# A fused attention and softmax-gated layer on one core: float16 parts in the first product, a three-part sum handed to VectorE, and a new instruction order

## The chip, the core and the metric

The kernel runs on one core of a Trainium2 chip. The core has five engines that run side by side, each with its own in-order queue: TensorE (PE in the profile, its weight loads PEld), VectorE (DVE), ScalarE (ACT), GpSimd (POOL) and SyncE (SP), which here only issues DMAs. Engines wait for one another through semaphores. PSUM holds the results of TensorE, SBUF everything else. The metric is the device time of one execution in microseconds; lower is better. Times given are medians of several runs.

## The reference

Two layers follow each other. The first mixes seven neighbouring rows of x with softmaxed weights, one weight per head (8 heads of 24 columns) and tap; the second is a gated layer with a layer norm inside.

```python
# x: (8, 4160, 192), weight_gen: (8, 4160, 8, 7)
w = exp(weight_gen - max); w = w / (sum(w) + 1e-9)
out[b, s, h, :] = sum over k of w[b, s, h, k] * x_pad[b, s + k, h, :]
# then, on 33280 rows of 192 columns:
h = x @ w_in                                  # 192 -> 1024
e = exp(h - max(h)); sm = e / (sum(e) + 1e-9)
solu = h * sm
ln = (solu - mean) / sqrt(var + 1e-6) * g_ln
return ln @ w_out                             # 1024 -> 192
```

The weights of the second layer arrive as 64-bit floats and are turned into 32-bit ones on the chip at the start.

## The kernel before, in words

Each of 128 partitions holds a run of 260 consecutive rows, so one "tile" t is one row of each partition, 128 rows in all, and the kernel works on 260 tiles. x and the tap weights are loaded in chunks: one of 4 tiles, two of 8, then fifteen of 16 (`starts`). Four tiles make a group.

For a chunk: `load_w`, `load_x` (four DMAs, SP queue), `softmax_taps` (steps t0 to t6, line 102: max on DVE, subtraction on POOL, exponential on ACT, sum on DVE, + 1e-9 on ACT, reciprocal on DVE, product on POOL), and `norm_x` (steps v00 to v5, line 136: squares of x on ACT with their sum, then a few one-column operations that end in an upper limit for the chunk's h, used as a scale).

For a group: `attention` (line 171) runs wholly on POOL. It multiplies the seven shifted windows of x with the taps (line 174), adds parts 3, 4, 5 to 0, 1, 2 (line 180), which leaves four, and adds these pairwise into the two parts of the tile `half` (line 182; `half` has two buffers). `last_sum` (line 428) adds the two parts on DVE with a reduction (line 433) into `a`; ACT copies a piece of it (line 439).

For two tiles: TensorE transposes `a` (line 450), ACT rounds it to fp32r as `x_hi` (line 458), DVE subtracts to get the remainder `x_lo` (line 479).

For a tile: the first product (line 483) makes h, 128 x 1024, in one of three PSUM tiles named h, from high and low parts of x and w_in: x_hi·w_hi + x_hi·w_lo + x_lo·w_hi, once for the last 64 rows of w_in (line 491, `wb`, both halves of h side by side in the array) and once for the first 128 (line 494, `wa`). Then come the negated row maximum on DVE (line 505), the exponential on ACT with its sum (line 509), h·e·scale on DVE with its sum, written over h (line 515), squares on ACT (line 521), a float16 high half on ACT (line 528) and a low half on DVE (line 532), a DMA transpose (line 540), the second product in float16, 24 matmuls of 192 columns (line 580), and the scaled output on ACT (line 591). Six small steps per group (`scales`, lines 544 to 571, f0 to f5) make the output scale. The scale of h, the squares, the high half and the low half all read the same PSUM tile; it is free for the next product when squares and low half are done.

At the start three pieces of w_in and four of w_out are converted (`float_of_double`, line 232, steps a, b and c; scratch in the same three PSUM tiles h), rounded into `wa_hi`, `wa_lo`, `wb_hi`, `wb_lo` (`first_rows`, `last_rows`), and a norm of w_in is taken (`norm_of_first`, lines 282 to 299, result `column`).

The order of everything behind the first few loads comes from a planner, `issue_order` (line 660). It holds a list of steps, each with an engine, a cost in ns and the steps that it waits for, plays them through, and at each moment gives a free engine the ready step with the lowest key, the tile number plus an offset from the table `URGENCY` (line 645). The list of steps that it returns is the order in which the kernel issues its instructions; each engine then runs its own in that order.

Of the kernel before, what the change touches and what calls it, by code (L numbers as in the profile page):

```python
# [26 lines left out]
def tile_kernel(ctx: ExitStack, tc: tile.TileContext, x, weight_gen, w_in, w_out, g_ln, out):  # L27
    nc = tc.nc
# [73 lines left out]
    def softmax_taps(c, step):  # L102
# [8 lines left out]
        if step == 0:  # L111
            nc.vector.tensor_reduce(m, w3, axis=AX.X, op=ALU.max)
        elif step == 1:
            nc.gpsimd.tensor_tensor(
                out=w3, in0=w3, in1=m.unsqueeze(2).broadcast_to(wide), op=ALU.subtract
            )
        elif step == 2:
            nc.scalar.activation(w3, w3, AF.Exp)
        elif step == 3:
            nc.vector.tensor_reduce(m, w3, axis=AX.X, op=ALU.add)  # L120
        elif step == 4:
            nc.scalar.activation(y, m, AF.Copy, bias=1e-9)
        elif step == 5:
            nc.vector.reciprocal(y, y)
        elif step == 6:
            nc.gpsimd.tensor_tensor(
                out=w3, in0=w3, in1=y.unsqueeze(2).broadcast_to(wide), op=ALU.mult
            )
# [5 lines left out]
    SUM, LN, NORM, LIMIT, SCALE, EPS, EPS_Z = (slice(n, n + 1) for n in range(7))  # L134

    def norm_x(c, step, part=0):
# [12 lines left out]
        elif step == 1:  # L149
            row_of[c] = small.tile([P, 7], F32, name="row", bufs=5)  # L150
# [3 lines left out]
        elif step == 2:  # L154
            row = row_of[c]
            nc.scalar.activation(row[:, LN], row[:, SUM], AF.Ln, bias=floor)
            nc.scalar.activation(row[:, NORM], row[:, LN], AF.Exp, scale=0.5)
        elif step == 3:
            row = row_of[c]
            nc.scalar.activation(row[:, LIMIT], row[:, NORM], AF.Copy, bias=0.5, scale=column)  # L160
        elif step == 4:
            nc.vector.reciprocal(row_of[c][:, SCALE], row_of[c][:, LIMIT])
        elif step == 5:
            row = row_of[c]
            nc.scalar.activation(row[:, EPS], row[:, SCALE], AF.Copy, scale=1e-3 * FF**1.5)
            nc.scalar.activation(row[:, EPS_Z], row[:, SCALE], AF.Copy, scale=1e-12 * FF**1.5)
# [4 lines left out]
    def attention(xt, wt, t, n, half):  # L171
# [7 lines left out]
        )  # L179
        nc.gpsimd.tensor_tensor(out=pr[:, :3], in0=pr[:, :3], in1=pr[:, 3:6], op=ALU.add)  # L180
# [43 lines left out]
    minus = const.tile([P, P], F32R, name="minus")  # L224
    nc.vector.tensor_scalar_mul(minus, ident, -1.0)

    for step in range(TAP_STEPS):
        softmax_taps(0, step)
# [37 lines left out]
    wa_hi = const.tile([P, FF], F32R, name="wa_hi")  # L266
    wa_lo = const.tile([P, FF], F32R, name="wa_lo")
    wb_hi = const.tile([P, FH], F32R, name="wb_hi")
    wb_lo = const.tile([P, FH], F32R, name="wb_lo")

    def last_rows(step):
        if step < 3:
            first["b"] = float_of_double("b", raw_b, FH, step)
        elif step == 3:
            nc.scalar.copy(wb_hi, first["b"])
        elif step == 4:
            nc.vector.tensor_tensor(
                out=wb_lo, in0=first["b"], in1=wb_hi.bitcast(F32), op=ALU.subtract
            )


    def norm_of_first(step):
# [14 lines left out]
        elif step == 6:  # L297
            nc.scalar.activation(column, first["total"][:, 8:9], AF.Ln, scale=1.05 * FF)
            nc.scalar.activation(column, column, AF.Exp, scale=0.5)

    def first_rows(f, step):
# [3 lines left out]
        elif step == 3:  # L305
            nc.scalar.copy(wa_hi[:, fs], first[f])
        elif step == 4:
            nc.vector.tensor_tensor(
                out=wa_lo[:, fs], in0=first[f], in1=wa_hi.bitcast(F32)[:, fs], op=ALU.subtract
# [107 lines left out]

    def attend(t):
        n = group(t)
        c = max(n for n in range(NCHUNK) if starts[n] <= t)  # L420
        half = att.tile([P, 2, TG, D], F32, name="half", bufs=2)[:, :, :n]
        half_of[t] = half
        attention(xs[c], ws[c], t - starts[c], n, half)
# [32 lines left out]
    def high_x(t):  # L456
        hi = small.tile([P, 2, 2, P], F32R, name="x_hi", bufs=2)
# [3 lines left out]
    def subtract_high(t):  # L461

        pa, hi = x_parts[t]
        for n in range(2):
            nc.tensor.matmul(
                pa[:, n], minus, hi[:, n], start=False, stop=n == 1, skip_group_check=True
            )

    def low_x(t):
        pa, hi = x_parts.pop(t)  # L470
        lo = small.tile([P, 2, 2, P], F32R, name="x_lo", bufs=2)
        nc.scalar.copy(lo, pa)
        for i in range(2):
            xt_of[t + i] = hi[:, :, i, :], lo[:, :, i, :]

    def low_x_on_vector(t):
        pa, hi = x_parts.pop(t)
        lo = small.tile([P, 2, 2, P], F32R, name="x_lo", bufs=2)
        nc.vector.tensor_tensor(out=lo, in0=pa, in1=hi.bitcast(F32), op=ALU.subtract)  # L479
# [24 lines left out]
    def maximum(t):  # L504
        nc.vector.tensor_reduce(stat(t, NMAX), h_of[t], axis=AX.X, op=ALU.max, negate=True)  # L505

    def exponentials(t):
        e = big.tile([P, FF], F32, name="e")
        nc.scalar.activation(e, h_of[t], AF.Exp, bias=stat(t, NMAX), accum_out=stat(t, Z))  # L509
# [92 lines left out]
    def at_chunk(op, *args):  # L602
# [4 lines left out]
        xhi=high_x, xn=subtract_high, xlo=low_x, xld=low_x_on_vector, mm1=first_product,  # L607
# [21 lines left out]
    for n in range(7):  # L629
# [10 lines left out]
    for op, t in issue_order(RUN, starts, group, stat_group, LOADS):  # L640
# [19 lines left out]
def issue_order(run, starts, group, stat_group, loads):  # L660

    PE, DVE, ACT, SP, POOL = range(5)
    SAME, CROSS = (25, 127, 143, 0, 102), 130
    free = [3000, 5900, 5000, 12000, 9050]
    steps, number = [], {}  # L670

    def add(name, t, engine, cost, *after, ready=0):
        number[name, t] = len(steps)
# [4 lines left out]


    parts = ["a0", "b", "a1", *(f"c{f}" for f in range(4))]  # L680
    for n, part in enumerate(parts):
        w_in, size = n < 3, 512 if n < 3 else 384
        at = (9000, 10500, 12000)[n] if w_in else 15000
        before = () if w_in else (f"{parts[n - 3]}4", "n" + {"a0": "0", "a1": "1", "b": "2"}[parts[n - 3]]) if n < 6 else ("q00",)
        if n:
            before += (parts[n - 1] + "0",)
# [3 lines left out]
        if w_in:  # L690
            once(part + "3", ACT, 190 + 0.75 * size, part + "2")
            once(part + "4", DVE, 60 + 1.04 * size, part + "3")
            once("n" + {"a0": "0", "a1": "1", "b": "2"}[part], DVE, 60 + 1.04 * size, part + "2")
        else:
            f = n - 3
            once(f"q{f}0", ACT, 700, part + "2")
            once(f"q{f}1", PE, 660, f"q{f}0", *([f"q{f - 1}1"] if f else ["n6"]))
# [6 lines left out]
    once("n3", ACT, 100, "n0", "n1", "n2")  # L704
    once("n4", PE, 220, "n3")
    once("n5", DVE, 70, "n4")
    once("n6", ACT, 400, "n5")
# [19 lines left out]
    def add_norms(c, t):  # L727
        add("v1", t, DVE, 70, *parts_of(c), *parts_of(c - 1), ("f5", starts[c - 4] - 1 if c > 4 else -1))
        add("v2", t, ACT, 420, ("v1", t))
        add("v3", t, ACT, 190, ("v2", t), ("n6", 0))  # L730
        add("v4", t, DVE, 80, ("v3", t))
        add("v5", t, ACT, 240, ("v4", t))

    add("v00", 0, ACT, 1800, ready=9000)
    add_norms(0, 0)
    for c in range(1, len(starts) - 1):
        t, before = starts[c], starts[c - 1] if c > 1 else -1
        short = starts[c + 1] - t < 16
# [5 lines left out]
        whole = starts[c + 1] - t == 16  # L744
        for part in range(4 if whole else 1):
            size = 830 if whole else 1800
            if c > 1:

                load = min(part + 1, loads - 1) if whole else loads - 1
                add(f"v0{part}", t, ACT, size, (f"lx{load}", t))  # L750
            else:
                add(f"v0{part}", t, ACT, size, ready=15000)
        add_norms(c, t)
        n = (starts[c + 1] - t) * 8
        on = (DVE, POOL, ACT, DVE, ACT, DVE, POOL)
        wide = 60 + 7.3 * n
        costs = (wide, 13.5 * n, 100 + 6 * n, wide, 100 + n, 60 + 6.3 * n, 13.5 * n)
        for k in range(7):
            if k:
                add(f"t{k}", t, on[k], costs[k], (f"t{k - 1}", t))  # L760
            elif c > 1:
                add("t0", t, on[k], costs[k], ("lw", t), ("t6", before))
            else:
                add("t0", t, on[k], costs[k], ready=12000)

# [159 lines left out]
```

## Time and profile before

| what | value |
|---|---|
| median of 3 runs | 1348.01 us (1347.25 to 1348.76) |
| profiled execution, span from first to last instruction | 1345.8 us |
| instructions | 25810 |
| mean granted TensorE clock | 0.994 |
| 66 products of line 174 on POOL | 631.6 us |
| 66 additions of line 180 on POOL | 333.0 us |
| 66 additions of line 182 on POOL | 225.8 us |
| moved by DMA | 210.31 MB, mean 156 GB/s |

No own time is listed for the profiled execution; its span is 2.2 us below the median of the runs. In a row of the profile that groups instructions, `x64` is the count, the two numbers behind the bar are the busy time in us and the mean of one in ns, and what follows the second bar is the idle time of the engine just before them with the engine that ended it. In a row of the waits the three numbers are the total in us, how often, and the longest. In a row of the timeline the first two are start and duration in us. A row of windows gives for each engine busy us and a count, then the clock, the share of the DMA engines and GB/s.

### The profile page before, as it was taken

What the parts mean: (1) busy time and instruction counts of PE and PEld (TensorE: products, weight loads), DVE (VectorE), ACT (ScalarE), POOL (GpSimd) and SP (SyncE); (2) the same over time, 40 slices, a digit from 0 to 9 for tenths busy, and PEclk for the clock granted to TensorE, in tenths of its full rate; (3) what the DMA queues carried; (4) which work ended last, traced back from release to release, by engine and by line L of the source; (5) the groups of instructions that cost most, each with busy time, mean ns of one, the idle gap of its engine ahead of it and who ended that gap; (6) DMA issues with size and microseconds to landing.
All of it is one profiled execution on the core that took longest, in us unless ns stands there. A gap on an engine that the chain in (4) does not pass through costs nothing.

```text
span 1345.8 us, 25810 instructions
## 1 busy us (share of the span) xinstructions
PE 1246.8 (93%) x9900; PEld 970.8 (72%) x9900; DVE 1210.2 (90%) x1588; ACT 1162.8 (86%) x2318; POOL 1247.7 (93%) x241
## 2 busy tenths in 40 slices
PE   0588899999999999999999999999999999999997
PEld 0365677777777777777777777777777777777776
DVE  5988899999999999999999999999999999889994
ACT  3778889889898988989898998989898898988886
POOL 5989899999999999999999999999999999999930
PEclk9899999999999999999999999999999999999999
DMA  5277668797886889688797968878787877976776
GB/s 180 74 159 169 139 134 201 123 207 137 155 179 134 196 137 208 125 179 163 129 202 140 191 140 180 162 128 203 140 193 137 183 150 138 183 134 123 133 134 130
DMA packets 565307, 210.31 MB, mean 156 GB/s; under 512 B 544456, under 2 KB 545864, under 8 KB 565184
## 3 DMA queue, kind: packets, MB, share of 16 engines
q1 hardware_dynamic: 563208, 206.55, 75.7%
q10 hardware_dynamic: 1976, 2.12, 0.6%
q8 instruction: 78, 1.28, 0.4%
q14 instruction: 45, 0.37, 0.1%
HBM read 46.15 MB, written 25.56 MB: 53 GB/s over the span
## 4 chain that ended last, share of the span: by engine, by line
ACT 43%; DVE 35%; issue 11%; PE 7%; DMA 2%; POOL 1%; SPq 0%; ACTq 0%; POOLq 0%
ACT hl L528 12%; ACT e L521 12%; DVE h L515 11%; DVE hl L532 11%; ACT e L509 9%; DVE stats L505 5%; DVE a L433 4%; ACT junk L145 3%; PE po L580 3%; PE h L494 2%; ACT x_hi L458 2%; ACT ot L591 2%; DMA hlT<-hl 2%; PE h L491 1%; DVE x_lo L479 1%
## 5 line engine op out<-in xcount | busy, mean ns | idle before, releaser
L174 POOL TENSOR_TENSOR pr<-xt,wt 128x5376 f32<-128x5376 f32 (+1 forms) x66 | 631.6, 9569 | 2.7
L580 PE MATMUL po<-w_hl,hlT 128*128 128x192 f16 x6192 | 555.1, 246 | 17.3 <-ACT ot L591 12.6
L580 PEld LDWEIGHTS <-hlT 128*128 128x128 f16 x6240 | 505.9, 98 | 83.2 <-issue 75.5
L515 DVE SCALAR_TENSOR_TENSOR h<-h,row,e 128x1024 f32<-128x1024 f32 x260 | 333.8, 1285 | 19.1 <-ACT e L509 16.9
L528 ACT ACTIVATE hl<-h 128x1024 f16<-128x1024 f32 x260 | 266.0, 1029 | 98.4 <-DVE h L515 55.4
L532 DVE SCALAR_TENSOR_TENSOR hl<-h,hl 128x1024 f16<-128x1024 f32 x260 | 316.5, 1218 | 36.8 <-ACT e L521 34.4
L180 POOL TENSOR_TENSOR pr<-pr 128x2304 f32<-128x2304 f32 (+1 forms) x66 | 333.0, 5045 | 5.2
L505 DVE TENSOR_REDUCE stats<-h 128x1 f32<-128x1024 f32 x260 | 316.3, 1217 | 3.9 <-PE h L494 3.3
L509 ACT ACTIVATE e<-h,stats 128x1024 f32<-128x1024 f32 x260 | 293.3, 1128 | 16.1 <-DVE stats L505 15.5
L521 ACT ACTIVATE e<-h,stats 128x1024 f32<-128x1024 f32 x260 | 293.0, 1127 | 1.1 <-DVE hl L532 1.0
L494 PE MATMUL h<-wa_hi,x_hi 128*128 128x512 f32 x520 | 234.0, 450 | 0.0
L182 POOL TENSOR_TENSOR half<-pr 128x1536 f32<-128x1536 f32 (+1 forms) x66 | 225.8, 3421 | 5.2
L494 PE MATMUL h<-wa_lo,x_hi 128*128 128x512 f32 x520 | 206.4, 397 | 0.0
L494 PE MATMUL h<-wa_hi,x_lo 128*128 128x512 f32 x520 | 205.9, 396 | 0.0
L494 PEld LDWEIGHTS h<-wa_hi,x_hi 128*128 128x128 f32 x520 | 98.1, 189 | 107.1 <-issue 95.5
L491 PE MATMUL h<-wb_hi,x_hi 64*128 64x512 f32 x520 | 131.0, 499 | 17.1 <-DVE hl L532 11.2
L433 DVE TENSOR_REDUCE a<-half 128x768 f32<-128x1536 f32 (+1 forms) x66 | 117.2, 1776 | 0.0
L591 ACT ACTIVATE ot<-po,stats 128x192 f32<-128x192 f32 x258 | 112.4, 436 | 3.6 <-PE po L580 3.6
L494 PEld LDWEIGHTS h<-wa_hi,x_lo 128*128 128x128 f32 x520 | 98.4, 189 | 23.2
L494 PEld LDWEIGHTS h<-wa_lo,x_hi 128*128 128x128 f32 x520 | 99.0, 190 | 12.0
L491 PE MATMUL h<-wb_hi,x_lo 64*128 64x512 f32 x520 | 104.2, 395 | 0.0
L450 PE MATMUL pa<-ident,a 128*128 128x128 f32 x520 | 81.2, 278 | 23.9 <-DVE x_lo L479 13.2
(89 smaller groups left out, 1072.0 us busy)
## 6 DMA issues: line engine op xcount, KB each, us to landing
out_dram<-ot SPq DMA_DIRECT2D x65, 384.0 KB, 3.3
xt<-in_x_dram SPq DMA_DIRECT2D x30, 576.0 KB, 4.8
xt<-in_x_dram SPq DMA_DIRECT2D x30, 480.0 KB, 4.4
wt<-in_weight_gen_dram SPq DMA_DIRECT2D x15, 448.0 KB, 4.8
hlT<-hl SPq DMA_TRANSPOSE x260, 4.7
xt<-in_x_dram SPq DMA_DIRECT2D x3, 384.0 KB, 4.6
raw_a<-in_moe_w_in_dram ACTq DMA_DIRECT2D x2, 512.0 KB, 7.4
raw<-in_moe_w_out_dram ACTq DMA_DIRECT2D x1, 768.0 KB, 12.2
```

The source lines that it names most:

```text
L174: nc.gpsimd.tensor_tensor(out=window(pr, 0, [(TG * D, K), (HG, n * H), (1, HG)]), in0=window(xt, t * D, [(D, K), (HG, n * H), (1, HG)]), i ...
L180: nc.gpsimd.tensor_tensor(out=pr[:, :3], in0=pr[:, :3], in1=pr[:, 3:6], op=ALU.add)
L182: nc.gpsimd.tensor_tensor(out=half, in0=window(pr, 0, [(2 * TG * D, 2), (D, n), (1, D)]), in1=window(pr, TG * D, [(5 * TG * D, 2), (D, n), ...
L491: nc.tensor.matmul(h[:, fs], lhs[rows, 1, :], rhs[rows], start=n == 0, stop=False)
L494: nc.tensor.matmul(h[:, fs], lhs[:, 0, :], rhs[:, fs], start=False, stop=n == 2)
L505: nc.vector.tensor_reduce(stat(t, NMAX), h_of[t], axis=AX.X, op=ALU.max, negate=True)
L509: nc.scalar.activation(e, h_of[t], AF.Exp, bias=stat(t, NMAX), accum_out=stat(t, Z))
L515: nc.vector.scalar_tensor_tensor(out=h, in0=h, scalar=row(t, SCALE), in1=e, op0=ALU.mult, op1=ALU.mult, accum_out=stat(t, M))
L521: nc.scalar.activation(e_of.pop(t), h_of[t], AF.Square, bias=stat(t, M), scale=-float(FF), accum_out=stat(t, Q),)
L528: nc.scalar.activation(hl[:, 0, :], h_of[t], AF.Copy, scale=2.0**14)
L532: nc.vector.scalar_tensor_tensor(out=hl[:, 1, :], in0=h_of[t], scalar=2.0**14, in1=hl[:, 0, :], op0=ALU.mult, op1=ALU.subtract,)
L580: nc.tensor.matmul(po[:, :D], hlT[:, half * NJ + j, :], w2_hl[:, j, w, :], start=n == 0, stop=n == len(terms) - 1,)
```

## The change

1. The first product uses float16 parts in place of fp32r ones. To keep the numbers in range, the taps of a chunk are divided by a multiple of that chunk's x norm (`UNIT`), w_in by a multiple of its own norm with the sign turned (`unit_w`), and h is multiplied back by `BACK`.
2. The row maximum on DVE becomes a multiplication of h by `BACK`, written over h, that accumulates a minimum; the exponential takes scale -1.
3. In every other group (t // 4 odd) POOL adds to three parts instead of two, and DVE's reduction sums three. `half` has room for three parts.
4. The planner is split in two, its costs and some waits are changed (the taps' step t4 waits for v2, the copies of w_in for n7, the maximum for v3), and `URGENCY` has new values for every step. Every step keeps its engine.

```diff
@@ softmax_taps, norm_x
-            nc.scalar.activation(y, m, AF.Copy, bias=1e-9)
+            row = row_of[c]
+            nc.scalar.activation(y, m, AF.Identity, bias=row[:, UNIT_Z], scale=row[:, UNIT])
...
+            nc.scalar.activation(row[:, UNIT], row[:, NORM], AF.Copy, bias=2.0**-22, scale=2.0**-15)
+            nc.scalar.activation(row[:, UNIT_Z], row[:, UNIT], AF.Copy, scale=1e-9)
...
-            nc.scalar.activation(row[:, LIMIT], row[:, NORM], AF.Copy, bias=0.5, scale=column)
+            nc.scalar.activation(row[:, BACK], row[:, UNIT], AF.Copy, scale=column)
+            nc.scalar.activation(row[:, LIMIT], row[:, BACK], AF.Copy, bias=-0.5, scale=-(2.0**30))
@@ attention, attend
+        if parts == 3:
+            nc.gpsimd.tensor_tensor(out=half, in0=pr[:, :3], in1=pr[:, 3:6], op=ALU.add)
+            nc.gpsimd.tensor_tensor(out=half[:, 2], in0=half[:, 2], in1=pr[:, 6], op=ALU.add)
+            return
...
+    def three(t):
+        return t // TG % 2 == 1
...
-        half = att.tile([P, 2, TG, D], F32, name="half", bufs=2)[:, :, :n]
+        parts = 3 if three(t) else 2
+        half = att.tile([P, 3, TG, D], F32, name="half", bufs=2)[:, :parts, :n]
@@ w_in parts (wa_hi, wa_lo, wb_hi, wb_lo now F16)
-            nc.scalar.copy(wa_hi[:, fs], first[f])
+            nc.scalar.activation(wa_hi[:, fs], first[f], AF.Copy, scale=unit_w)
...
-            nc.vector.tensor_tensor(
-                out=wa_lo[:, fs], in0=first[f], in1=wa_hi.bitcast(F32)[:, fs], op=ALU.subtract
+            nc.vector.scalar_tensor_tensor(
+                out=wa_lo[:, fs], in0=first[f], scalar=unit_w, in1=wa_hi[:, fs],
+                op0=ALU.mult, op1=ALU.subtract,
             )
@@ norm_of_first
+            nc.scalar.activation(column, column, AF.Copy, bias=2.0**-22, scale=2.0**-15)
+            nc.scalar.activation(unit_w, column, AF.Copy, scale=-1.0)
+        elif step == 7:
+            nc.vector.reciprocal(unit_w, unit_w)
@@ high_x, low_x (x_hi, x_lo now F16)
-        nc.vector.tensor_tensor(out=lo, in0=pa, in1=hi.bitcast(F32), op=ALU.subtract)
+        nc.vector.tensor_tensor(out=lo, in0=pa, in1=hi, op=ALU.subtract)
@@ maximum, exponentials
-        nc.vector.tensor_reduce(stat(t, NMAX), h_of[t], axis=AX.X, op=ALU.max, negate=True)
+        h = h_of[t]
+        nc.vector.tensor_scalar(
+            h, h, row(t, BACK), 3.0e38, op0=ALU.mult, op1=ALU.min, accum_out=stat(t, NMAX)
+        )
...
-        nc.scalar.activation(e, h_of[t], AF.Exp, bias=stat(t, NMAX), accum_out=stat(t, Z))
+        nc.scalar.activation(
+            e, h_of[t], AF.Exp, bias=stat(t, NMAX), scale=-1.0, accum_out=stat(t, Z)
+        )
@@ planner, the waits
-            once(part + "3", ACT, 190 + 0.75 * size, part + "2")
+            once(part + "3", ACT, 280 + 0.75 * size, part + "2", "n7")
...
+            if k == 4:
+                after.append(("v2", t))
...
-        add("max", t, DVE, 1140, ("mm1", t), ("f5", stats_of[t - 24] if t >= 24 else -1))
+        add("max", t, DVE, 1211, ("mm1", t), ("f5", stats_of[t - 24] if t >= 24 else -1), ("v3", starts[chunk_of(t)]))
```

In the last_rows of `wb` the same edit stands as in those of `wa`. Of chunk 0 only the first four tap steps are still issued ahead of the planner's order; the last three come in its order.

More of the change, by code (lines that the diff above doesn't have):

```diff
@@ L149, in norm_x @@
         elif step == 1:
[L150 removed]
+            row_of[c] = small.tile([P, 10], F32, name="row", bufs=5)
             nc.vector.tensor_reduce(
@@ L223, in tile_kernel @@
     column = const.tile([P, 1], F32, name="column")
-    minus = const.tile([P, P], F32R, name="minus")
-    nc.vector.tensor_scalar_mul(minus, ident, -1.0)
-    for step in range(TAP_STEPS):
+    unit_w = const.tile([P, 1], F32, name="unit_w")
+    for step in range(TAP_STEPS - 3):
         softmax_taps(0, step)
@@ L265, in tile_kernel @@
     first = {}
[L266 to L269, printed above, removed]
+    wa_hi = const.tile([P, FF], F16, name="wa_hi")
+    wa_lo = const.tile([P, FF], F16, name="wa_lo")
+    wb_hi = const.tile([P, FH], F16, name="wb_hi")
+    wb_lo = const.tile([P, FH], F16, name="wb_lo")
     def last_rows(step):
@@ L628, in tile_kernel @@
         ops[f"f{n}"] = at(scales, n)
-    for n in range(7):
+    for n in range(8):
         ops[f"n{n}"] = once(norm_of_first, n)
@@ L657, with plan @@
+    v01=232.5, v02=215.4, v03=-140.7, v1=-139.9, v2=154.7, v3=-54.4, v4=178.2, v5=249.3, xT=-134.3,
+    xhi=133.1, xld=7.4,
 )
-def issue_order(run, starts, group, stat_group, loads):
+def plan(run, starts, group, stat_group, loads, three):
     PE, DVE, ACT, SP, POOL = range(5)
-    SAME, CROSS = (25, 127, 143, 0, 102), 130
-    free = [3000, 5900, 5000, 12000, 9050]
-    steps, number = [], {}
+    steps = []
     def add(name, t, engine, cost, *after, ready=0):
-        number[name, t] = len(steps)
@@ L703, in issue_order @@
     once("p4", ACT, 660, "p6")
-    once("n3", ACT, 100, "n0", "n1", "n2")
+    once("n3", ACT, 192, "n0", "n1", "n2")
     once("n4", PE, 220, "n3")
     once("n5", DVE, 70, "n4")
-    once("n6", ACT, 400, "n5")
+    once("n6", ACT, 800, "n5")
+    once("n7", DVE, 70, "n6")
     for half in "01":
@@ L725, in parts_of @@
         return [(f"v0{n}", starts[c]) for n in range(4 if starts[c + 1] - starts[c] == 16 else 1)]
[L727 to L736, printed above, removed]
+    for c in range(len(starts) - 1):
         t, before = starts[c], starts[c - 1] if c > 1 else -1
-        short = starts[c + 1] - t < 16
+        size = starts[c + 1] - t
+        whole = size == 16
         if c > 1:
@@ L743, in issue_order @@
                 add(f"lx{n}", t, SP, 1540, (f"lx{n - 1}", t))
-        whole = starts[c + 1] - t == 16
         for part in range(4 if whole else 1):
-            size = 830 if whole else 1800
             if c > 1:
                 load = min(part + 1, loads - 1) if whole else loads - 1
-                add(f"v0{part}", t, ACT, size, (f"lx{load}", t))
+                add(f"v0{part}", t, ACT, 870 if whole else 1650, (f"lx{load}", t))
             else:
-                add(f"v0{part}", t, ACT, size, ready=15000)
-        add_norms(c, t)
-        n = (starts[c + 1] - t) * 8
-        on = (DVE, POOL, ACT, DVE, ACT, DVE, POOL)
[L756 to L764, printed above, removed]
+                add(f"v0{part}", t, ACT, 1900, ready=15000 if c else 9000)
+        add("v1", t, DVE, 70, *parts_of(c), *parts_of(c - 1), ("f5", starts[c - 4] - 1 if c > 4 else -1))
+        add("v2", t, ACT, 1000, ("v1", t))
+        add("v3", t, ACT, 590, ("v2", t), ("n6", 0))
+        add("v4", t, DVE, 80, ("v3", t))
+        add("v5", t, ACT, 350, ("v4", t))
+        n = size * 8
+        wide = 60 + 7.8 * n
+        on = (DVE, POOL, ACT, DVE, ACT, DVE, POOL)
+        costs = (wide, 13.4 * n, 100 + 5.8 * n, wide, 150 + n, 60 + 6.3 * n, 13.4 * n)
+        for k in range(7) if c else range(4, 7):
+            after = [(f"t{k - 1}", t)] if k and (c or k > 4) else []
+            if k == 4:
+                after.append(("v2", t))
+            if k == 0 and c > 1:
+                after += [("lw", t), ("t6", before)]
+            add(f"t{k}", t, on[k], costs[k], *after, ready=12000 if c == 1 and not k else 0)
     groups = [t for t in range(run) if group(t)]
@@ L836, in issue_order @@
             count[i] += 1
-    key = [t + URGENCY.get(name, 0) for name, t, *_ in steps]
+    key = [round(t + URGENCY.get(name, 0), 6) for name, t, *_ in steps]
     later, now = [[] for _ in free], [[] for _ in free]
@@ L841, in issue_order, with gap @@
             heapq.heappush(later[step[2]], (ready[i], key[i], i))
+    def gap(e, to):
+        if e == to and to != SP:
+            return SAME[e]
+        return FROM_PE if e == PE and to != SP else CROSS
     queue = data = 0
```

157 lines of the change are left out of this document (73 added, 84 removed).

## The prediction, made before the changed kernel was run

> **What bounds the kernel now.** I read the totals first, then the steady stretch, then who waits, then the end. The first rows are the page's totals and the chain by engine.
>
> ```profile
> PE 1246.8 (93%) x9900; PEld 970.8 (72%) x9900; DVE 1210.2 (90%) x1588; ACT 1162.8 (86%) x2318; POOL 1247.7 (93%) x241
> ...
> ACT 43%; DVE 35%; issue 11%; PE 7%; DMA 2%; POOL 1%; SPq 0%; ACTq 0%; POOLq 0%
> ```
>
> Three engines are about full and ACT stands at 86%; the chain alone would point at ACT and VectorE (DVE), so shares do not settle it. The steady stretch follows (busy us and share of each engine in 260 to 1060 us, then in a piece near the end), and below it the count of line 505, one row maximum per tile, in 1000 us.
>
> ```profile
> 260.00:1060.00 800.00, 780.48 (x6251) 607.62 (x6249) 741.90 (x955) 717.41 (x1427) 788.51 (x144) 1.00 0.81 162
> 1260.00:1300.00 40.00, 39.39 (x323) 31.25 (x321) 37.55 (x50) 35.01 (x66) 30.04 (x6) 1.00 0.69 138
> ```
> ```profile
> 260.00:1260.00 1000.00, 249.62 (x206) 1.00 0.80 160
> ```
>
> 206 tiles in 1000 us are 4.854 us a tile. Per tile POOL is then busy 788.51/800 x 4.854 = 4.78, PE 4.74, DVE 4.50, ACT 4.35. What each waits for in that stretch:
>
> ```profile
> DVE stats L552 <- ACT e L521: 25.8, 31, 1.1
> ...
> DVE hl L532 <- ACT e L521: 17.4, 31, 0.6
> ...
> ACT e L509 <- DVE stats L505: 11.7, 10, 1.2
> DVE h L515 <- ACT e L509: 11.2, 22, 0.8
> ...
> POOL wt L126 <- DVE stats L552: 3.4, 8, 0.5
> ```
>
> POOL waits 3.4 us in 800; DVE waits 25.8 + 17.4 + 11.2 = 54.4 us, always for ACT, 0.33 us for each of the 165 tiles. So POOL sets the pace and DVE has time to wait in. POOL's own rows at the end of its work show the same:
>
> ```profile
> 1234.91 9.71 POOL L174 TENSOR_TENSOR pr<-xt,wt 128x5376 f32<-128x5376 f32 x1
> ...
> 1253.44 9.73 POOL L174 TENSOR_TENSOR pr<-xt,wt 128x5376 f32<-128x5376 f32 x1
> ...
> 1271.97 9.70 POOL L174 TENSOR_TENSOR pr<-xt,wt 128x5376 f32<-128x5376 f32 x1
> ...
> 1286.95 3.48 POOL L182 TENSOR_TENSOR half<-pr 128x1536 f32<-128x1536 f32 x1
> ```
> ```profile
> L580 PEld LDWEIGHTS <-hlT 128*128 128x128 f16 x6240 | 505.9, 98 | 83.2 <-issue 75.5 <-DMA hlT<-hl 6.9
> L515 DVE SCALAR_TENSOR_TENSOR h<-h,row,e 128x1024 f32<-128x1024 f32 x260 | 333.8, 1285 | 19.1 <-ACT e L509 16.9
> ...
> L505 DVE TENSOR_REDUCE stats<-h 128x1 f32<-128x1024 f32 x260 | 316.3, 1217 | 3.9 <-PE h L494 3.3
> ...
> L182 POOL TENSOR_TENSOR half<-pr 128x1536 f32<-128x1536 f32 x64 | 222.2, 3471 | 5.0
> ...
> L433 DVE TENSOR_REDUCE a<-half 128x768 f32<-128x1536 f32 x64 | 115.3, 1801 | 0.0
> ...
> L494 PEld LDWEIGHTS h<-wa_hi,x_hi 128*128 128x128 f32 x520 | 98.1, 189 | 107.1 <-issue 95.5
> ...
> L145 ACT ACTIVATE junk<-xt 128x768 f32<-128x768 f32 x60 | 51.6, 859 | 5.6 <-DMA xt<-in_x_dram 5.1
> ...
> L114 POOL TENSOR_TENSOR wt<-wt,wm 128x896 f32<-128x896 f32 x15 | 26.6, 1772 | 9.7 <-DVE row L151 6.3 <-DVE wm L112 3.4
> L126 POOL TENSOR_TENSOR wt<-wt,wy 128x896 f32<-128x896 f32 x15 | 26.5, 1766 | 4.7 <-DVE stats L552 3.9 <-ACT ot L591 0.8
> ...
> L165 ACT ACTIVATE row<-row 128x1 f32<-128x1 f32 x18 | 4.2, 236 | 0.6 <-DVE row L162 0.6
> ...
> L182 POOL TENSOR_TENSOR half<-pr 128x768 f32<-128x768 f32 x2 | 3.6, 1814 | 0.2
> ...
> L246 DVE TENSOR_SCALAR h<-h 128x512 int32<-128x512 int32 x3 | 2.1, 696 | 0.1
> L260 DVE TENSOR_TENSOR h<-frac,h 128x512 f32<-128x512 f32 x3 | 2.1, 695 | 0.1
> ...
> L433 DVE TENSOR_REDUCE a<-half 128x384 f32<-128x768 f32 x2 | 1.9, 954 | 0.0
> ```
>
> A group of four tiles takes POOL 18.53 us (1234.91 to 1253.44 to 1271.97), 4.63 a tile, and the two tap passes of a chunk (lines 114 and 126, 1.77 each) add 3.54/16 = 0.22: 4.85, the measured pace. Behind POOL's last addition, which ends at 1290.43, the span still has 55.4 us.
>
> **The change, part by part.** *POOL.* In every other group the last addition (line 182) shrinks from 128x1536, 3.471 us, to 128x768, which two first half-groups show at 1.814. That is 1.657 less in each of 32 groups, 53.0 us in all, 0.207 a tile: POOL's floor falls from 4.85 to 4.65.
>
> *DVE, the sum of three parts.* Line 433 reads 2304 elements in place of 1536. From 768 to 1536 it went from 0.954 to 1.801, so 768 more cost 0.847; over eight tiles 0.106 a tile, 27 us in all.
>
> *DVE, the maximum.* Line 505 becomes a multiplication that writes the tile back to PSUM and accumulates the minimum. No row has that form. The nearest are line 505 itself (1.217) and line 515, which also writes 1024 elements and accumulates, with one input more (1.285). I take 1.285, 0.068 a tile more, because the write-back is what the two rows differ in; upwards 0.21 (the 0.14 us accumulator read of line 515, below, not overlapping the next instruction). Downwards a one-input form could pass two elements at a time; lines 246 and 260, a tensor_scalar and a tensor_tensor on 512 PSUM elements, took 696 and 695 ns, so one input is no faster than two here; the rival is priced below.
>
> DVE becomes 4.50 + 0.106 + 0.068 = 4.68. Part of that is drain that only a wait uncovers:
>
> ```profile
> 617.36 1.28 DVE L515 SCALAR_TENSOR_TENSOR h<-h,row,e 128x1024 f32<-128x1024 f32 x1
> 618.56 0.14 DVE L515 DVE_READ_ACCUMULATOR h<-h,row,e 128x1 f32 x1
> ...
> 623.19 1.22 DVE L505 TENSOR_REDUCE stats<-h 128x1 f32<-128x1024 f32 x1
> 624.32 1.21 DVE L532 SCALAR_TENSOR_TENSOR hl<-h,hl 128x1024 f16<-128x1024 f32 x1
> ```
>
> Line 505 started at 623.19, is shown for 1.22, and the next instruction started after 1.13. Line 515's accumulator read lies under the next instruction. The 84 waits of the stretch uncover some 0.09 us each, 0.04 a tile, so a DVE without waits needs 4.64. POOL's new floor is 4.65: the change brings the two level.
>
> *PE.* The first product streams nine times 512 columns (the two 64-row halves run side by side), 4608 in all; line 580 streams 24 times 192, 4608 as well, in float16.
>
> ```profile
> 615.75 0.50 PE L491 MATMUL h<-wb_hi,x_hi 64*128 64x512 f32 x2
> ...
> 618.15 2.15 PE L580 MATMUL po<-w_hl,hlT 128*128 128x192 f16 x24
> ```
>
> Today the first product takes 618.15 - 615.75 = 2.40 us, line 580 2.15. In float16 the first product should come near the latter, since its loads shrink from 189 ns (line 494) to the 98 of line 580: 0.25 less a tile, bounds 0 and, with fewer loads than line 580, 0.4. A loss has no row for it. PE goes from 4.74 to 4.49. At zero it would stay at 4.74 and be the bound; that is in the third rival.
>
> *ACT.* Casts to float16 (line 528 does such a cast today) replace casts to fp32r of the same size: nothing; the same holds for DVE's remainders. A chunk gets three more one-column activations (0.236, line 165): 0.04 a tile, 4.35 to 4.39. That stays 0.3 below the new pace and is hidden by it; without that cover it would cost 11 us.
>
> *New waits.* A chunk's taps are now divided with its x norm, so step t4 waits for v2, hence for the x loads and four squares, and POOL's products wait for t6. Queued behind t6 on POOL is all attention of the chunk. A chunk's x buffer comes free a whole chunk earlier (16 x 4.7 = 75 us), against some 9 us of loads and squares:
>
> ```profile
> xt<-in_x_dram SPq DMA_DIRECT2D x30, 576.0 KB, 4.8
> ```
>
> The four loads overlap (4.8 each to landing) and four squares are 4 x 0.86. I cost it at nothing, and up to 9 us a chunk if an order puts v2 late. The maximum waits for v3 of its chunk; DVE's queue stands behind it, and v3 follows v2 at once. The DMA queue, busy 0.81, rises to about 0.83.
>
> *The start.* Two edits, told by these rows:
>
> ```profile
> 17.08 0.58 POOL L126 TENSOR_TENSOR wt<-wt,wy 128x224 f32<-128x224 f32 x1 [13.26 <-DVE wy L124]
> ```
> ```profile
> 9.15 1.79 ACT L145 ACTIVATE junk<-xt 128x1920 f32<-128x1920 f32 x1
> ...
> 37.30 0.20 ACT L299 ACTIVATE column<-column 128x1 f32<-128x1 f32 x1
> ```
> ```profile
> 34.85 0.68 DVE L284 TENSOR_REDUCE sq<-h 128x1 f32<-128x512 f32 x1
> ```
> ```profile
> 45.84 0.79 PE L491 MATMUL h<-wb_hi,x_hi 64*128 64x512 f32 x2
> ```
>
> The first taps now follow the square of x (ends near 11.0), a sum, five short activations and a reciprocal, then the POOL pass: seven short steps near line 165's 0.236 and 0.58 on POOL, some 2.5 us with the hops between engines (an estimate), so 13.5 at best against 17.08 today; if the reciprocal is queued behind the weight conversion on DVE (a dozen passes near 0.70, lines 246 and 260), some 8 us later than now. I take no change. The float16 weights wait for unit_w, known three short steps behind line 299 (37.5), and through it for all three parts' maxima (line 284, the last of them ending at 35.5). Copies and remainders of three parts (six steps near 0.7) then end near 42, still ahead of the first product at 45.84; but they also hold the scratch tiles that the w_out conversion needs. I take +3 us, bounds -4 and +10.
>
> *The end.* PE is busy 39.39 of 40 us there; about eight products by 0.25 give -2 (0 to -4).
>
> **The sum.** A bound engine here is busy 98.6% (POOL) and PE, in the loop with ACT and DVE, still 97.6%. With DVE between 4.64 and 4.68 and about 1% idle I take 4.71 a tile. About 245 tiles run at that pace: (4.854 - 4.71) x 245 = 35.3. Span 1345.8 - 35.3 + 3 - 2 = 1311.5. The median of the runs, 1348.01, lies 2.2 above the profiled span, so the time is 1313.7, rounded 1314.
>
> **The rivals.** *POOL alone stays the bound,* because DVE follows without idling: 4.65, 0.204 x 245 = 50 less, 1345.8 - 50 + 1 + 2.2 = 1299. For it: POOL hardly waits today. Against: DVE would have to run without a gap while it now waits for ACT 84 times in 165 tiles.
>
> *The new maximum passes two elements at a time.* By line 433 an element costs (1801 - 954)/768 = 1.10 ns; half of 1024 are 0.56 us, DVE falls to 4.1, and POOL alone sets the pace: 1299 again. Lines 246 and 260 speak against it. The Trainium skill (VectorE: DVE Perf Modes, the perf-mode tier table) lists tensor_scalar with a PSUM operand at up to twice the plain rate; the same page, on why PSUM operands drop a tier, says plain rate for fp32, and the two rows side with that.
>
> *Half of DVE's waits stay, or PE gives little back:* 4.66 + 0.165 = 4.82, or 4.74 at 98.6% = 4.81. Then 0.04 x 245 = 10 less: 1339. For it: the waits are round trips DVE, ACT, DVE of one tile, and nothing shortens ACT.
>
> *Slower: DVE's waits are needed, not slack.* If all 0.33 stay, 4.66 + 0.33 = 4.99, 0.136 x 245 = 33 more: 1382. It decides from 0.19 us of waits a tile on (4.854 - 4.66). For it: the chain is 78% ACT and DVE, and the added work lands on DVE. Against: POOL is the engine that never waits, so DVE has to idle 0.35 a tile whatever it does.
>
> *The parts do not shorten POOL* (two dependent additions with a gap between): no time won there, DVE busier, but still under 4.85: 1348, within the measurement.
>
> **How the numbers follow.** Forecast 0.60, POOL alone 0.11, two elements 0.03, half of the waits 0.14, slower 0.09, nothing won 0.03. The likeliest gives 1314. The range 1297 to 1338 reaches to the cases at 1299 and nearly to the one at 1339, and takes in a start off by 10; it leaves out the slow case. About 0.2% (2.7 us) can be told from no change: faster 0.87 (one hundredth of the half-waits case is given away to slower), same 0.03, slower 0.10.
>
> **What would show it.** Right: line 182 in two sizes, about 3.47 and 1.8; the three-part sums near 2.65 and the new maximum near 1.28; DVE at 98% or more of the steady stretch and its waits for ACT under 0.1 us a tile; POOL slightly below its 98.6%; first-product loads near 98 ns. Wrong: DVE still waiting for ACT 0.2 us a tile or more, PE at 97% with unchanged gaps, POOL waiting at line 126 or for DVE's sums, or a first product well after 56 us.

## The result, and the profile after

The changed kernel takes 1324.9 us (median of 4 runs, 1323.8 to 1330.45) against 1348.22 for the kernel before on the same chip: a ratio of 0.983, with a 95% interval of 0.9815 to 0.9846. The forecast was 1314, in a range of 1297 to 1338. The profiled execution has a span of 1323.2 us, 22.6 less than before.

Where the 22.6 us were won is read from the starts of the row maxima (line 505 before, 511 after). The maximum of tile 20 starts at 160.7 us where it started at 166.6: 5.9 are won at the start. From tile 20 to tile 244 it takes 1073.5 where it took 1088.8: 15.3, or 0.068 a tile (4.792 against 4.861; the prediction's 4.854 came from a count of 206 tiles in 1000 us). The rest of the span gives 1.4.

The page's totals and the chain by engine, the kernel after:

```profile
PE 1170.4 (88%) x9900; PEld 781.8 (59%) x9900; DVE 1244.9 (94%) x1848; ACT 1174.0 (89%) x2374; POOL 1190.7 (90%) x241
...
DVE 59%; issue 15%; ACT 11%; DMA 8%; PE 6%; SPq 1%; DVEq 0%; POOL 0%; ACTq 0%; POOLq 0%
```

The chain has moved from ACT and DVE mostly to DVE, and loads of x stand in it now (DMA 8%, was 2%). The steady stretch, 260 to 1060 us, in the columns PE, PEld, DVE, ACT, POOL, clock, DMA share, GB/s:

```profile
260.00:1060.00 800.00, 738.36 (x6274) 493.27 (x6273) 768.43 (x1127) 729.92 (x1468) 758.40 (x147) 0.99 0.77 167
```

DVE is the fullest engine with 96.1%, POOL fell from 98.6 to 94.8% and PE from 97.6 to 92.3%. The new instructions, in the groups by line:

```profile
L511 DVE TENSOR_SCALAR_CACHE_REDUCE h<-h,row 128x1024 f32<-128x1024 f32 x260 | 334.4, 1287 | 6.1 <-PE h L499 6.1
...
L453 DVE TENSOR_REDUCE a<-half 128x768 f32<-128x2304 f32 x32 | 89.3, 2791 | 0.0
...
L499 PEld LDWEIGHTS <-x_hi 128*128 128x128 f16 x1040 | 80.7, 98 | 174.7 <-issue 114.1
...
L188 POOL TENSOR_TENSOR half<-half,pr 128x768 f32<-128x768 f32 x32 | 58.1, 1814 | 2.5
```

Line 188 is the short addition (1.814 us, as forecast), line 453 with 2304 elements the three-part sum (2.791, forecast 2.65), line 511 the new maximum (1.287, forecast 1.285), and the float16 weight loads take 98 ns. The parts cost what they should. What does not fit is who waits, in 260 to 1060 us:

```profile
ACT junk L148 <- DMA xt<-in_x_dram: 33.7, 17, 4.1
...
DVE hl L542 <- ACT hl L538: 27.5, 15, 3.6
POOL wt L127 <- DVE wy L125: 20.5, 6, 6.3
...
POOL wt L127 <- DMA out_dram<-ot: 12.2, 4, 3.6
```

Before, the waits of this stretch name no transfer. Now ACT stands 33.7 us at the squares of x (line 148) until a load lands, in 17 waits of 2 us, some 3 us in every chunk (16 tiles, 77 us), and DVE 27.5 us at its low half (line 542) for ACT's high half (line 538). POOL waits 32.7 us at its second pass over the taps (line 127), about 3 us a chunk too; but the profile shows no wait of DVE for POOL's sums in this stretch, so POOL follows DVE here and does not set the pace. One place where ACT waits and DVE behind it, ACT first:

```profile
500.39 0.21 ACT L172 ACTIVATE row<-row 128x1 f32<-128x1 f32 x1
503.30 0.84 ACT L148 ACTIVATE junk<-xt 128x768 f32<-128x768 f32 x1 [2.69 <-DMA xt<-in_x_dram]
...
504.14 1.01 ACT L538 ACTIVATE hl<-h 128x1024 f16<-128x1024 f32 x1
```
```profile
502.60 0.14 DVE L511 DVE_READ_ACCUMULATOR h<-h,row 128x1 f32 x1
505.18 1.23 DVE L542 SCALAR_TENSOR_TENSOR hl<-h,hl 128x1024 f16<-128x1024 f32 x1 [2.44 <-ACT hl L538]
```

The square was next in ACT's queue, and its data came 2.69 us after ACT had come to it. The high half stood behind the square, and DVE, done at 502.7, waited 2.44 us for it. SyncE's queue (issues) and the DMA share (last but one column) around it:

```profile
492.12 0.57 SPq L90 DMA_DIRECT2D xt<-in_x_dram  x1
492.74 0.43 SPq L96 DMA_DIRECT2D wt<-in_weight_gen_dram  x1
...
498.06 0.42 SPq L90 DMA_DIRECT2D xt<-in_x_dram  x1
498.59 6.42 SPq L550 DMA_TRANSPOSE hlT<-hl  x2
505.06 0.57 SPq L90 DMA_DIRECT2D xt<-in_x_dram  x1
...
509.21 1.19 SPq L90 DMA_DIRECT2D xt<-in_x_dram  x1
```
```profile
485.00:490.00 5.00, 4.41 (x41) 3.16 (x39) 5.00 (x7) 4.91 (x9) 4.92 (x2) 1.00 0.00 0
490.00:495.00 5.00, 4.39 (x38) 2.81 (x37) 5.00 (x11) 4.64 (x8) 4.92 (x2) 1.00 1.12 173
495.00:500.00 5.00, 5.00 (x44) 3.34 (x43) 5.00 (x11) 4.97 (x12) 2.50 (x2) 1.00 1.13 304
500.00:505.00 5.00, 4.86 (x40) 2.94 (x39) 2.74 (x5) 2.31 (x8) 4.92 (x2) 1.00 1.09 253
505.00:510.00 5.00, 2.91 (x20) 2.78 (x20) 4.82 (x7) 5.00 (x10) 5.00 (x1) 0.74 1.33 223
```

The loads of one chunk (four of x, one of weights) go out between 492 and 509, with transposes between them on the same queue. In the 5 us before, the DMA engines show no packets (0.00); in the 20 us after that their packets take 1.09 to 1.33 of the time there is, where the mean is 0.77. The stall costs PE as well: in the last 5 us it is busy 2.91, at a granted clock of 0.74, and the 24 matmuls of line 590 behind its wait take 3.77 us, where those of the tile before took 2.14.

Full DMA engines are not new, though. In the kernel before, where the loads of a chunk go out between 517 and 533, the same columns read:

```profile
520.00:525.00 5.00, 5.00 (x39) 3.86 (x39) 5.00 (x7) 3.99 (x8) 5.00 (x1) 1.00 1.03 301
525.00:530.00 5.00, 5.00 (x42) 3.89 (x40) 4.88 (x7) 4.01 (x8) 4.92 (x2) 1.00 1.23 255
530.00:535.00 5.00, 4.47 (x39) 3.45 (x38) 4.43 (x6) 5.00 (x11) 4.92 (x2) 1.00 1.00 214
```

Nor do single loads of x take longer from issue to landing in 260 to 1060 us: a median of 4.4 us (at most 7.2), where it was 4.7 (5.7). What is new is where the squares stand in ACT's queue. Before, the squares of a chunk start 1.5 to 2.5 us behind the landing of the load that they need (the medians of the four squares, in the ten chunks whose loads begin in the steady stretch up to 1000 us). In the changed kernel the first and the third start as theirs lands (both medians 0.0). The new order leaves them no margin, and the loads are issued one at a time, behind transposes.

### The profile page after: what moved, and what is told of

It is laid out like the page before. It is cut to its first block, busy times and chain, and to the rows that moved or that the text cites. A ratio compares the mean times of both kernels' runs of the same rounds, so it can differ in the third digit from the quotient of the medians.

```text
span 1323.2 us, 26171 instructions
## 1 busy us (share of the span) xinstructions
PE 1170.4 (88%) x9900; PEld 781.8 (59%) x9900; DVE 1244.9 (94%) x1848; ACT 1174.0 (89%) x2374; POOL 1190.7 (90%) x241
## 4 chain that ended last, share of the span: by engine, by line
DVE 59%; issue 15%; ACT 11%; DMA 8%; PE 6%; SPq 1%; DVEq 0%; POOL 0%; ACTq 0%; POOLq 0%
DVE hl L542 16%; DVE h L511 16%; DVE h L525 12%; DVE a L453 8%; DMA xt<-in_x_dram 7%; DVE x_lo L484 4%; ACT hl L538 3%; ACT e L531 3%; PE po L590 3%; ACT e L517 3%; PE h L499 1%; SPq L550 1%; DVE wm L120 1%; PE h L496 1%; ACT x_hi L478 1%
## 5 line engine op out<-in xcount | busy, mean ns | idle before, releaser
L511 DVE TENSOR_SCALAR_CACHE_REDUCE h<-h,row 128x1024 f32<-128x1024 f32 x260 | 334.4, 1287 | 6.1 <-PE h L499 6.1
L499 PE MATMUL h<-wa_hi,x_hi 128*128 128x512 f16 x520 | 201.6, 388 | 0.0
L499 PE MATMUL h<-wa_lo,x_hi 128*128 128x512 f16 x520 | 198.9, 383 | 0.0
L499 PE MATMUL h<-wa_hi,x_lo 128*128 128x512 f16 x520 | 198.6, 382 | 0.0
L190 POOL TENSOR_TENSOR pr<-pr 128x2304 f32<-128x2304 f32 (+1 forms) x34 | 167.6, 4929 | 2.7
L187 POOL TENSOR_TENSOR half<-pr 128x2304 f32<-128x2304 f32 x32 | 162.4, 5075 | 2.5
L496 PE MATMUL h<-wb_hi,x_hi 64*128 64x512 f16 x520 | 102.6, 390 | 52.8 <-DVE hl L542 32.8
L453 DVE TENSOR_REDUCE a<-half 128x768 f32<-128x2304 f32 (+1 forms) x66 | 148.2, 2245 | 0.0
L192 POOL TENSOR_TENSOR half<-pr 128x1536 f32<-128x1536 f32 (+1 forms) x34 | 113.8, 3347 | 2.7
L496 PE MATMUL h<-wb_hi,x_lo 64*128 64x512 f16 x520 | 100.4, 381 | 0.0
```

Source lines behind the costliest of these rows:

```text
L453: nc.vector.tensor_reduce(columns(t)[:, :, :D], half.rearrange("p j t d -> p t d j"), axis=AX.X, op=ALU.add)
L496: nc.tensor.matmul(h[:, fs], lhs[rows, 1, :], rhs[rows], start=n == 0, stop=False)
L499: nc.tensor.matmul(h[:, fs], lhs[:, 0, :], rhs[:, fs], start=False, stop=n == 2)
L511: nc.vector.tensor_scalar(h, h, row(t, BACK), 3.0e38, op0=ALU.mult, op1=ALU.min, accum_out=stat(t, NMAX))
```

## The experiments

All times are medians; the ratio is to the kernel before on the same chip, whose medians in the three sets of runs were 1348.63, 1349.26 and 1349.04 us. Theory A: the squares of x are too early, or the loads too late, and ACT's in-order queue stands. Theory B: DVE's waits are round trips that the loop through ACT needs (the prediction's third and fourth rivals). Theory C: x loads and transposes get in each other's way, in the queue or in the DMA engines, so that moving the one makes the other late; it stands in the expectation of the early loads and was widened for the later runs.

### Squares later

```diff
+    moved = {(n, t) for n in ("v00", "v01", "v02", "v03", "v1", "v2", "v3") for t in starts[3:-1]}
...
+    for x in moved:
+        i, left = key[x][0], by
+        while left:
+            i += 1
+            left -= engine[order[i]] == engine[x] and order[i] not in moved
+        key[x] = (i, 1 + key[x][0])
```

> Kernel: the changed one; in its order the four squares of each x chunk, and the steps v1, v2 and v3 that follow them, stand four places later in their engine's queue. Theory A (ScalarE stands at a square whose x load has not landed, 33.7 us in the steady 800, and VectorE behind it at line 542, 27.5 us): most of these waits go, VectorE gets busier than 98% in the steady stretch, a tile goes from 4.79 to about 4.65, and the time falls by 20 to 30 us to about 1300. Theory B (VectorE's waits are round trips that the loop through ScalarE needs): the wait only changes its name, VectorE stays near 96%, and the time stays within 5 us of 1325.

1330.59 us, ratio 0.9859 (0.9833 to 0.9884). Not faster: the waits at line 542 fell from 27.5 to 10.3 us, and those at the squares (line 148) from 33.7 to 3.2, but the pace is 4.821 a tile: DVE's other, smaller waits for ACT rose from 1.0 to 16.1 us. So A in its simple form falls; with this run alone B stands.

### Loads early

```diff
+    late = {(f"lx{n}", t) for n in (1, 2, 3) for t in starts[3:-1]}
...
+        if x in late:
+            continue
+        out.append(x)
+        if x[0] == "lx0" and x[1] in starts[3:-1]:
+            out += [(f"lx{n}", x[1]) for n in (1, 2, 3)]
```

> Kernel: the changed one; in its order the second to fourth x load of a chunk are issued on SyncE's queue right behind the first, ahead of the transposes that stood between them; nothing else moves. Theory A (the squares wait because the loads are issued late): the squares find their data, the time falls by 20 to 30 us to about 1300. Theory B (loop through ScalarE): no change, within 5 us of 1325. Theory C (the loads share one DMA queue with the transposes, which were put between them on purpose): the transposes land later, TensorE waits at line 590 for them, and the gain is eaten, time 1320 or more.

1322.84 us, ratio 0.9817 (0.9793 to 0.9841), not to be told from the changed kernel. The waits say why, in 260 to 1060 us:

```profile
ACT hl L538 <- DMA hlT<-hl: 33.3, 12, 4.5
DVE hl L542 <- ACT hl L538: 30.0, 11, 4.1
```

The wait for x is gone. In its place stands, with almost the same sum, a wait of the high half for the DMA transpose that must free one of three hl buffers. The loads of x now land in 5.8 us (median; it was 4.4) and the slowest transpose in 11.8 (it was 9.1). That is theory C, except that its late transpose holds up ACT at line 538 and not PE at line 590: something lands late, and whichever ACT instruction needs it next holds up the queue, and DVE behind it.

### Two parts, three parts

```diff
-        parts = 3 if three(t) else 2
+        parts = 2
```

```diff
-        parts = 3 if three(t) else 2
+        parts = 3 if t >= TG else 2
```

> Kernel: the changed one with two parts in every group again, order and float16 kept. Theory A and B alike: GpSimd needs 4.85 us a tile again and is the bound, VectorE gets 0.12 a tile back that it cannot use; time 1340 to 1350, so the three-part sum is what the change lives on. A rival (the float16 product and the order bring the gain, GpSimd's share is hidden): time stays near 1325.

> Kernel: the changed one with three parts in every group behind the first tiles, order kept: GpSimd falls by another 0.2 us a tile, VectorE rises by 1.01/8 = 0.126 a tile. Theory A and B: VectorE is the bound now, the 0.126 appears in full, 250 x 0.126 = 31 us, time about 1355. A rival (GpSimd is still the bound at 4.63 and its waits): time falls below 1325.

Two parts everywhere: 1332.52, ratio 0.9882 (0.9866 to 0.9897), 4.815 a tile, POOL busy 98.9% of the steady stretch. POOL is the bound again, but the expectation was too high: in the new order POOL needs 77.0 us a chunk instead of 77.8. So of the change's gain only some 8 us came from the three-part sum. The waits for x are there in this run as well, at POOL's pace: 36.5 us at line 148, and 29.5 at line 542 for line 538. Three parts everywhere: 1349.62, ratio 1.0004 (0.999 to 1.0018), 4.897 a tile (its profiled execution, 1355.84, was the slowest of ten), 0.105 more than the changed kernel where DVE got 0.126 more to do. DVE decides, though it is not full (96.7%).

### Almost no x traffic

```diff
+            r1 = r1 if c < 5 else r0 + 1
             nc.sync.dma_start(xv[:, r0:r1, :], x_run[:, t0 - HALO + r0 : t0 - HALO + r1, :])
```

> Kernel: the changed one without most of its x traffic: from the sixth chunk on, each of the four loads of a chunk brings a single row and the other rows keep what an older chunk left there; instructions, order and waits stay. Theory C (at each chunk's loads the DMA engines are full for some 25 us, so x lands late or transposes land late, and ScalarE's in-order queue stands at a square or at the float16 half, VectorE behind it): the waits of line 148 and of line 542 for ScalarE fall to almost nothing, VectorE is over 98% busy, a tile takes about 4.65, time about 1295 to 1303. Theory B (round trips between VectorE and ScalarE are the limit): other waits take their place, time above 1315.

1288.87 us, ratio 0.9553 (0.9536 to 0.957). Instructions and order are the same, the bytes are not, and 36 us go. (The kernel leaves out most of x, so this is the time without these bytes and not a version of the layer.) The loads land in 2.9 us (median), and no square waits for one. The steady stretch:

```profile
260.00:1060.00 800.00, 761.24 (x6538) 508.14 (x6537) 797.86 (x1174) 760.89 (x1532) 787.94 (x151) 1.00 0.70 147
```

DVE is 99.7% busy; it waits for ACT at no place that counts. B falls: the loop can keep DVE full.

### Early loads and five buffers

```diff
-        hl = hl_of[t] = big.tile([P, 2, FF], F16, name="hl", bufs=3)
+        hl = hl_of[t] = big.tile([P, 2, FF], F16, name="hl", bufs=5)
```

> Kernel: loads_early with five buffers in place of three for the float16 halves that wait for their transpose. Theory C: loads_early took the wait for x away and put the wait for a transposed buffer (33.3 us at line 538) in its place; with two more buffers that wait goes too, and the time falls to about 1300. Theory B: stays within 5 us of 1322.8.

1285.59 us, ratio 0.9531 (0.9516 to 0.9546): all the work is done, and it beats both kernels, the one before by 4.7%. The steady stretch, DVE's longest wait that is left, and the landing times of the transposes:

```profile
260.00:1060.00 800.00, 761.67 (x6544) 509.10 (x6543) 798.45 (x1175) 760.96 (x1532) 788.36 (x153) 1.00 0.77 172
```
```profile
DVE a L453 <- POOL half L188: 1.1, 1, 1.1
```
```profile
DMA to landing us min/median/max: 3.6/4.0/11.3
```

The DMA share is that of the changed kernel (0.77), and where a chunk's loads go out, from 550 to 570, it is 1.09, with DVE busy for all of the 20 us. The slowest transpose takes 11.3 us, and nobody waits for it. DVE is busy 99.8%, a tile takes 4.628.

### Five buffers alone, loads from ACT's queue

```diff
-            nc.sync.dma_start(xv[:, r0:r1, :], x_run[:, t0 - HALO + r0 : t0 - HALO + r1, :])
+            nc.scalar.dma_start(xv[:, r0:r1, :], x_run[:, t0 - HALO + r0 : t0 - HALO + r1, :])
```

> Kernel: the changed one with five buffers for the float16 halves, nothing else. Theory C: no help alone, since here the wait is for x itself: within 4 us of 1325, the wait of line 148 stays near 30 us in the steady stretch. Theory B: no change either; this run only separates the buffer from the early loads.

> Kernel: the changed one with the x loads issued from ScalarE's queue in place of SyncE's; their places in the order stay. Theory C (it is the DMA engines that are full, not SyncE's queue): x lands hardly earlier, ScalarE pays about 0.5 us for each of four issues a chunk, time 1325 to 1340. A rival (SyncE's in-order queue, standing at transposes, issues the loads late): x lands earlier, the waits of line 148 go, time falls by 10 us or more.

Five buffers alone: 1332.42, ratio 0.9881 (0.9847 to 0.9916), the wait at line 148 at 39.0 us. The buffers help only with the loads out of the way. Loads from ACT's queue: 1326.85, ratio 0.9856 (0.9804 to 0.9908). The wait for x fell to 13.5 us, and 11.2 us of waiting for transposes came; the slowest transpose took 11.4 us, where it took 9.1. The Trainium skill (DMA: Bandwidth & Descriptors, Queues, rings and completion order) says that SP and ACT each own a row of rings on the same 16 engines, each of which takes turns between the rows that have work for it. The run is in line with that: the loads now land in 4.9 us (median; it was 4.4), 9.7 at most, and the other queue changes who is late and not the time.

### What each part is worth once the transfers are out of the way

Three edits of the version with early loads and five buffers (the last with four, and with its squares written in float16), and the early loads put into the kernel before.

```diff
-        parts = 3 if three(t) else 2
+        parts = 2
```

```diff
-        nc.vector.tensor_scalar(
-            h, h, row(t, BACK), 3.0e38, op0=ALU.mult, op1=ALU.min, accum_out=stat(t, NMAX)
-        )
+        nc.vector.tensor_reduce(stat(t, NMAX), h, axis=AX.X, op=ALU.min)
```

```diff
-    wa_hi = const.tile([P, FF], F16, name="wa_hi")
+    wa_hi = const.tile([P, FF], F32R, name="wa_hi")
...
-        hi = small.tile([P, 2, 2, P], F16, name="x_hi", bufs=2)
+        hi = small.tile([P, 2, 2, P], F32R, name="x_hi", bufs=2)
```

> Kernel: loads_early_hl5 with two parts in every group again. If the transfer stalls were all that hid the gain of the three-part sum: GpSimd needs 4 x 18.43 + 3.5 = 77.2 us a chunk, 4.83 a tile, against 4.635 in loads_early_hl5; time about 1285.6 + 245 x 0.19 = 1330 to 1335, so the three parts are worth about 45 us there and 7.6 us in the changed kernel as it stands. If not: 1290 to 1300.

> Kernel: loads_early_hl5 with the plain row minimum of line 511 (one reduction that writes nothing back, so h is not multiplied back; two later constants are smaller to keep the numbers in range). VectorE loses 0.07 us a tile. If VectorE alone is the bound: 250 x 0.07 = 17 us less, 1268. If GpSimd stands level with it (74.0 against 74.16 us a chunk): GpSimd's share becomes the limit and the time falls by no more than 4 us, 1282 to 1285.

> Kernel: loads_early_hl5 with fp32r in place of float16 parts in the first product (scaling kept), four buffers instead of five for the float16 halves and a float16 scratch tile for the squares, to make room. If TensorE gets its 0.25 us a tile back as the prediction had it: TensorE at 4.41 + 0.25 = 4.66 is above the 4.635 of the others and becomes the bound, time 1300 to 1315. If the float16 product saved nothing that counts: 1286 to 1290.

> Kernel: the kernel before with early loads and four buffers for the float16 halves, its order otherwise kept. GpSimd is the bound there and never waits for a transfer: time within 3 us of 1348. If transfer stalls cost that kernel too: 1335 or less.

Their steady stretches, in this order for the first three (same columns as above):

```profile
260.00:1060.00 800.00, 740.45 (x6279) 489.50 (x6276) 747.57 (x1127) 727.87 (x1468) 790.26 (x146) 0.99 0.73 166
```
```profile
260.00:1060.00 800.00, 762.73 (x6573) 510.11 (x6572) 791.74 (x1004) 757.10 (x1535) 790.60 (x153) 1.00 0.76 172
```
```profile
260.00:1060.00 800.00, 791.34 (x6382) 623.73 (x6384) 784.23 (x1145) 753.34 (x1496) 772.32 (x148) 1.00 0.74 169
```

Two parts: 1333.37 (0.9863 to 0.9908), POOL 98.8% busy, 48 us above 1285.59. The same kernel with three buffers and the late loads took 1332.52: with POOL as the bound, the waits for transfers cost nothing. Plain minimum (it leaves out the multiplication of h by `BACK`, so it serves for its time alone): 1279.86 (0.9471 to 0.9509), only 6 of DVE's 17 us show, since POOL, 98.8% busy, stands right behind. fp32r: 1320.15 (0.9769 to 0.9809), PE 98.9% busy, 4.753 a tile: 35 us, more than expected. PE busy per tile is 791.34/800 x 4.753 = 4.70 there and 761.67/800 x 4.628 = 4.41 with float16, 0.29 apart. The kernel before with early loads: 1352.37, ratio 1.0022 (1.0012 to 1.0032), 3 us slower and no gain; POOL was its bound and no transfer.

## Why the prediction was right, and where it was off

The direction holds, 1324.9 lies in the range, and POOL stopped being the bound as forecast, but the gain of the steady stretch was less than half of the forecast. That the time is only 11 us off is partly luck: some 20 us were missing in the steady stretch, and the start came out 9 us better than it was put.

- *POOL.* Forecast 1.657 us less for each of 32 groups; measured 3.443 and 1.814, 1.63 less. Right. That POOL paced the kernel before fits the two runs with two parts (POOL 98.9 and 98.8% busy).
- *DVE.* The new maximum was right to 0.002 us; it takes as long as line 525 with two inputs (1.287 and 1.286 us), so two elements at a time are ruled out here. The three-part sum was 0.14 us dearer than forecast, 4.5 us over 32 groups. The floor without waits, 4.64 a tile, is what the version with early loads and five buffers runs at (4.628, DVE 99.8% busy). "The change brings the two level" is right too: there POOL is 98.5% busy, and taking 17 us from DVE gains 6.
- *PE.* 0.25 less a tile was forecast, 0.29 is measured, and without it the fp32r run is bound by PE. It was no side effect: with fp32r PE is the bound at 4.753, whatever POOL and DVE could do.
- *The step that failed* is in the sum: "With DVE between 4.64 and 4.68 and about 1% idle I take 4.71 a tile." DVE idled 3.9%, 0.19 us a tile, and the pace was 4.792: 0.08 x 245 = 20 us lost. Its root is the paragraph on new waits. It costed the x loads at nothing, since they have a whole chunk's time, and asked only whether POOL's products and the maxima would wait for them. The loads are late for a square that stands in ACT's queue in front of work that DVE needs, and with early loads it is a transpose that lands late.
- *Where these waits come from.* They do not need the faster pace: the run with two parts, which keeps the new order, has them at 4.815 a tile, and the kernel before, at 4.861 and with DMA engines about as full, does not. The margins of the squares put them down to the new order; no run has the old order with the rest of the change. The pace decides what they cost: nothing while POOL is the bound (1332.52 with them, 1333.37 without), 39 us in the changed kernel. By the prediction's own signs the result lies between: DVE waits for ACT 0.17 us a tile (right was under 0.1, wrong from 0.2 on), and POOL does wait at the old line 126, now 127.
- *The rivals.* About half of the waits did stay, as in the rival at 1339, but not as round trips: without x traffic they are gone at once. The rival at 1299 needed a DVE without gaps, which was thought hard; it is there once transfers are out of the way: at 4.628 a tile, and with the earlier start, the time is 1285.59.
- *The start.* +3 us was forecast, and the first product does start 1.9 later (47.74 against 45.84 us). But the maximum of tile 20 came 5.9 earlier, so 6.7 were won between tile 0 (51.4 against 50.6) and tile 20. At 0.068 a tile, 20 tiles would give 1.4 of them. No run takes the rest apart: the new order and the moved tap steps both act there.

What stays open: why five buffers alone gave 1332.42, at or just above the changed kernel, and why moving the squares four places opened new waits; that any such shift makes other pairs meet is a guess, and only the sum of the waits was followed. Nor was it tested how much of each late landing is the queue, where a load stands behind transposes, and how much the engines.

## What to carry to other kernels

When a change takes the bound from one engine, look at what the others' slack was hiding: a wait that costs nothing while that engine is the bound comes into the sum when it is not. And when a change comes with a new order, read the margins of that order: how long after the landing of a transfer its first reader stands. A DMA share of 0.8 as a mean can be over 1 for 20 us in each period; read it in windows as short as the wait. A full stretch did no harm where the order left a margin behind each landing (the kernel before) or buffers for a late one (early loads and five buffers), so ask which in-order queue stands at the late transfer and what is behind it. If an edit removes a wait and the time stays, look for the wait of the same size beside it: here two edits, each worth nothing alone, were worth 39 us together.

## What the runs showed of the hardware

DVE ran 99.8% busy over 800 us, with ACT at 95.1%, PE at 95.2% and POOL at 98.5%; a static order can keep four engines there. An addition of 768 columns cost POOL 1.63 us less than one of 1536, and the same part, summed on DVE, cost DVE 1.01 more (2.791 against 1.780). A first product in fp32r parts cost PE 0.29 us a tile more than one in float16 with the same number of columns. In 260 to 1060 us of the changed kernel the granted TensorE clock fell to half five times, for 3.4 us (once 6.8), each time at an idle of PE of 2.2 to 4.5 us, though idles of 2.08 and 2.54 us went without; in the kernel before PE had no idle above 0.6 us in that stretch, and the clock never fell.
